# The second MoE stage's two projections as Strassen's seven block products over 384-token halves

## The chip, the cores and the metric

The kernel runs on one core of a Trainium2 chip. Five engines of the core work side by side and wait for each other through semaphores: TensorE (PE) multiplies matrices and writes the sums into PSUM, eight banks of 512 float32 columns on 128 partitions; VectorE (DVE) and ScalarE (ACT) do elementwise work and can read and write PSUM; GpSimd (POOL) does elementwise work in SBUF only; SyncE (SP) issues the DMAs. The metric is the time on the device in microseconds (us), less is better.

## What is computed

Attention over 2 x 768 tokens, then two MoE layers, each with one dense expert. The change touches only the second of them:

```python
def _moe_ref(x, w_in, w_out):           # 1536 tokens, 512 -> 2048 -> 512
    h = x @ w_in
    g = np.where(h >= 1, h, np.where(h <= -1, 0.0, (h + 1) ** 2 / 4.0))
    return (g @ w_out).astype(np.float32)

def _moe2_ref(x, w_gate, w_val, w_out): # 1536 tokens, 512 -> 1536 -> 512
    gate = 1.0 / (1.0 + np.exp(-(x @ w_gate)))
    val = x @ w_val
    return (gate * val @ w_out).astype(np.float32)
```

The weights come as float64. Every factor of a matmul is split in two float32r parts, a high one (the rounded value) and a low one (what the rounding lost), and a product is high x high + high x low + low x high: three matmuls for one.

## The kernel before

The attention part (`banded`, line 571 on) works on tiles of 112 queries; the first MoE layer's first stage runs between its tiles. After it comes `moe` (line 562): for each layer, each stage and each block of `TOK` = 512 tokens it calls `block` (line 404). A stage is a group of hidden chunks of 128 columns: four stages of four chunks in layer 1, four of three in layer 2 (`STAGES`, line 26). "The second stage" in this text means layer 2 as a whole.

`block` in layer 2 does this for each of its three chunks `f`: `proj("wg", f)` and `proj("wv", f)` each issue 12 matmuls of 512 columns (four 128-row parts of the model dimension times three products, lines 437 to 439) into one bank; ACT takes the sigmoid of the gate's bank (line 469); DVE multiplies it with the value's bank (line 472); the result is split into `gh` (a copy, lines 291, 293 or 295 by engine) and `gl` (a subtraction, line 298). Then the back projection: for each of four 128-token tiles, three chunks times three matmuls (lines 521 to 523), and a sum into `acc` in SBUF (line 536). In the last stage each finished tile is written out by a DMA of SP (line 546).

`load` (line 342) brings a weight chunk: a DMA of the float64 bits into `st`, then ACT rescales the high words (362), DVE clamps (365), shifts (368), restores the sign (371) and appends the low bits (374), and the chunk is split into its high and low part. Nineteen slots hold split chunks (`N_EARLY`, `N_LATE`), more than two stages of layer 2 need, so that later chunks are loaded while earlier ones are in use.

At the end of layer 1 the finished `acc` of a block is split into `xh` and `xl` (lines 540 to 543), on which layer 2 works.

The order of all this isn't the order of the calls. Every step is handed to a planner (`Plan`, line 117) with the engines that can do it, a duration for each, a due time, and what it reads and writes. `order` (line 158) runs through time: whenever an engine is free, it starts the step with the earliest due time among those that are ready and for whose new buffers there is room. `self.due` counts PE's work; elementwise steps get the due time of their matmul less `DRAIN` = 3.77. The instructions are then issued in that order; nothing is decided at run time, and each engine takes its instructions strictly in order. Buffers come from rings (`Ring`): all PSUM rings share the eight banks, and a ring of `n` buffers gives out buffer `i` when buffer `i - n` is done.

Of the kernel before, what the change touches and what calls it, by code (L numbers as in the profile page):

```python
# [25 lines left out]
STAGES = {1: (4, 4, 4, 4), 2: (3, 3, 3, 3)}  # L26
GROUPS = (512, 1024, 1536)
N_EARLY = 8
N_LATE = 19 - N_EARLY
G_BUFS = 6  # L30
PR_BUFS, PTS_BUFS, V_BUFS, C_BUFS = 6, 6, 6, 2
SC_BANKS, OT_BANKS, PT_BANKS, O_BANKS, H_BANKS = 4, 1, 2, 4, 5

# [65 lines left out]
class Ring:  # L99


    def __init__(self, n, make, banks=None):
        self.n, self.make, self.asked, self.taken, self.banks = n, make, [], 0, banks

# [12 lines left out]
class Plan:  # L117
# [40 lines left out]
    def order(self):  # L158
# [13 lines left out]
        running = []  # L172

        def room(o, t):
# [8 lines left out]
            return all(len(idle(b.ring.banks, t)) >= len(o.new) for b in o.new if b.ring.banks)  # L183
# [4 lines left out]
        def idle(banks, t):  # L188

            ends = [(0.0 if b is None else max(u.end for u in b.users), i) for i, b in enumerate(banks) if b is None or over(b, t)]  # L190
            return [i for _, i in sorted(ends)]
# [10 lines left out]
        while done < len(self.ops):  # L202
# [13 lines left out]
            for e in engines:  # L216
# [9 lines left out]
                for b in o.new:  # L226
                    b.ring.taken += 1
                    if b.ring.banks:
                        b.bank = idle(b.ring.banks, now)[0]
                        b.ring.banks[b.bank] = b  # L230
                t = begin(o, e)
# [14 lines left out]
    def run(self):  # L246
        order, end = self.order()
        for o in order:
            for b in o.new:
                b.ap = b.ring.make(b.bank) if b.ring.banks else b.ring.make()  # L250
            o.fn(o.eng) if o.pick else o.fn()
        return end


class Body:


    def __init__(self, ctx, tc, a, out, pre):
# [4 lines left out]
        self.stages = {}  # L263
        for layer, f in ((1, a["w1"].shape[0]), (2, a["wg"].shape[0])):
            ends = [sum(STAGES[layer][:i + 1]) for i in range(len(STAGES[layer]))]
            assert ends[-1] == f
            self.stages[layer] = [range(e - n, e) for e, n in zip(ends, STAGES[layer])]
# [3 lines left out]
        slots = self.pool(ctx, "w1p")  # L271
        self.early = [self.slot_tiles(slots, i) for i in range(N_EARLY)]
        g, tmp, wst = self.pool(ctx, "g"), self.pool(ctx, "tmp"), self.pool(ctx, "wst")
# [4 lines left out]
        ring = lambda pool, n, shape, dt, tag: Ring(n, lambda: pool.tile(shape, dt, tag=tag, name=tag, bufs=n))  # L278
        self.g_r = [ring(g, G_BUFS, [P, TOK], F32R, t) for t in ("gh", "gl")]
        self.t_r = [ring(tmp, 2, [P, TOK], F32, t) for t in ("r", "v")]  # L280
        self.o_r = self.bank_ring(O_BANKS)
        self.st_r = ring(wst, 3, [P, 512, 2], I32, "st")
        self.c_r, self.w_r = ring(wst, C_BUFS, [P, 512], F32, "c"), ring(wst, 2, [P, 512], F32, "w")
        self.h_r = self.bank_ring(H_BANKS)
        self.due = 0.0
        self.att_end = None
        self.weights()
# [20 lines left out]
    def bank_ring(self, n, parts=P, *shape):  # L308
# [9 lines left out]
        return Ring(n, view, self.banks)  # L318

    def slot_tiles(self, pool, i):  # L320
        return tuple(pool.tile([P, 512], F32R, name=f"w{x}{i}") for x in "hl")

    def later(self):
        if self.late is None:
            self.att.close()
            self.late = {"w": self.pool(self.ctx, "w2p")}
            self.late["slots"] = [self.slot_tiles(self.late["w"], N_EARLY + i) for i in range(N_LATE)]
        return self.late


    def weights(self):

        self.units, self.first = [], {}
        for layer, into, back in ((1, ("w1",), "w2"), (2, ("wg", "wv"), "wo")):
            for fs in self.stages[layer]:
                for nm, f in [(nm, f) for f in fs for nm in into] + [(back, f) for f in fs]:
# [677 lines left out]
```

## Time and profile before

| | |
|---|---|
| median of 3 runs | 658.73 us (657.57 to 660.29) |
| the profiled execution's span | 657.5 us |
| PE, DVE, ACT, POOL busy | 98%, 67%, 43%, 6% of the span |
| instructions | 9228, of them 3373 matmuls and 3373 weight loads |
| mean granted TensorE clock | 0.996 of 2.4 GHz |

A profile is one execution, taken by the hardware's profiler; its span goes from the first to the last instruction. A view by lines groups instructions; "idle before" is the time in which the engine waited for them, with what released it. Matmuls are pipelined: their recorded durations overlap, so their pace is the distance of their starts, which the view in order of time gives. DVE's and ACT's records overlap a little for the same reason.

### The profile page before, as it was taken

The page shows a single profiled execution, that of the slowest core. Times are in us where ns is not written, and L with a number is a line of the kernel's source. Part 1 is how long each engine was busy: PE and PEld are TensorE (multiplying, and loading weights), DVE is VectorE, ACT ScalarE, POOL GpSimd, SP SyncE. Part 2 cuts the span into 40 slices and gives each one's busy share as a digit, 9 for nine tenths or more (in the row PEclk, how much of TensorE's full clock was granted, in tenths as well). Part 3 has the DMA queues.
Part 4 walks back from the last instruction along what each step waited for, and adds up shares of the span by engine and source line. Part 5 has one row for each costly group of instructions (what it writes and reads, how often), then busy time and mean ns, then how long its engine had stood idle before and what let it go on. Part 6 is the DMA issues. An engine that isn't in the chain of part 4 may idle for free.

```text
span 657.5 us, 9228 instructions
## 1 busy us (share of the span) xinstructions
PE 645.8 (98%) x3373; PEld 527.9 (80%) x3373; DVE 439.0 (67%) x955; ACT 283.6 (43%) x614; POOL 40.3 (6%) x49
## 2 busy tenths in 40 slices
PE   8999999999999999999999999999999999999996
PEld 5677777888888888888888888888888888888885
DVE  5799998799998895789788902973278222222322
ACT  5899988556553442344445422441133111111110
POOL 0021111001010000000001100000000000000000
PEclk9899999999999999999999999999999999999999
DMA  6677555142443221122012300340011000001012
GB/s 189 204 224 214 165 171 167 33 146 80 160 129 96 97 94 34 33 96 97 32 33 96 123 7 0 127 147 16 0 44 55 0 1 0 1 0 65 1 64 69
DMA packets 28566, 54.43 MB, mean 83 GB/s; under 512 B 3296, under 2 KB 18400, under 8 KB 28512
## 3 DMA queue, kind: packets, MB, share of 16 engines
q1 hardware_dynamic: 28512, 53.75, 25.6%
q8 instruction: 28, 0.46, 0.3%
q14 instruction: 26, 0.21, 0.1%
HBM read 50.60 MB, written 3.15 MB: 82 GB/s over the span
## 4 chain that ended last, share of the span: by engine, by line
PE 90%; DVE 7%; DMA 1%; ACT 1%; issue 0%; DVEq 0%; ACTq 0%
PE bank L437 16%; PE bank L439 16%; PE bank L438 16%; PE bank L517 7%; PE bank L519 7%; PE bank L518 7%; PE bank L522 5%; PE bank L523 5%; PE bank L521 5%; PE bank L648 2%; DVE pr L651 2%; PE bank L688 2%; PE bank L665 2%; DMA qk<-in_qk 1%; DVE xl L298 1%; PE bank L711 0%
## 5 line engine op out<-in xcount | busy, mean ns | idle before, releaser
L437 PE MATMUL bank<-xh,wh 128*128 128x512 f32 x480 | 188.0, 392 | 0.0
L438 PE MATMUL bank<-xl,wh 128*128 128x512 f32 x480 | 187.1, 390 | 0.1
L439 PE MATMUL bank<-xh,wl 128*128 128x512 f32 x480 | 187.0, 390 | 0.0
L291 ACT ACTIVATE gh<-v 128x512 fp32r<-128x512 f32 x81 | 51.2, 632 | 137.8 <-DVE v L472 114.2
L437 PEld LDWEIGHTS bank<-xh,wh 128*128 128x128 f32 x480 | 90.2, 188 | 19.0 <-issue 0.3
L438 PEld LDWEIGHTS bank<-xl,wh 128*128 128x128 f32 x480 | 90.2, 188 | 18.8 <-DVE xl L298 0.4
L439 PEld LDWEIGHTS bank<-xh,wl 128*128 128x128 f32 x480 | 90.2, 188 | 18.7
L472 DVE TENSOR_TENSOR v<-r,bank 128x512 f32<-128x512 f32 x36 | 24.7, 686 | 104.1 <-PE bank L439 104.1
L536 DVE TENSOR_TENSOR acc<-bank,acc 128x512 f32<-128x512 f32 (+1 forms) x73 | 49.1, 683 | 44.2 <-PE bank L523 31.4
L517 PE MATMUL bank<-gh,wh 128*128 128x512 f32 x192 | 75.5, 393 | 0.0
L519 PE MATMUL bank<-gh,wl 128*128 128x512 f32 x192 | 74.8, 390 | 0.0
L518 PE MATMUL bank<-gl,wh 128*128 128x512 f32 x192 | 74.8, 390 | 0.0
L298 DVE TENSOR_TENSOR gl<-v,gh 128x512 fp32r<-128x512 f32 x83 | 57.0, 687 | 19.1 <-ACT gh L291 19.0
L362 ACT ACTIVATE c<-st 128x512 f32<-128x512 f32 x68 | 45.5, 671 | 33.1 <-DVE w L371 9.8
L657 ACT ACTIVATE pr<-pr,mx 112x256 f32<-112x256 f32 (+2 forms) x112 | 54.0, 487 | 10.5 <-DVE mx L651 10.1
L523 PE MATMUL bank<-wh,gl 128*128 128x512 f32 (+1 forms) x147 | 56.6, 385 | 0.0
L522 PE MATMUL bank<-wl,gh 128*128 128x512 f32 (+1 forms) x147 | 56.6, 385 | 0.0
L521 PE MATMUL bank<-wh,gh 128*128 128x512 f32 (+1 forms) x147 | 56.6, 385 | 0.0
L291 ACT ACTIVATE wh<-w 128x512 fp32r<-128x512 f32 x53 | 33.3, 630 | 48.3 <-PE bank L438 18.9
L469 ACT ACTIVATE r<-bank 128x512 f32<-128x512 f32 x36 | 21.5, 597 | 61.4 <-PE bank L439 61.3
L371 DVE SCALAR_TENSOR_TENSOR w<-c,w 128x512 int32<-128x512 int32 x68 | 47.7, 707 | 0.3
L374 DVE SCALAR_TENSOR_TENSOR w<-st,w 128x512 int32<-128x512 int32 x68 | 46.9, 693 | 0.4
(87 smaller groups left out, 770.4 us busy)
## 6 DMA issues: line engine op xcount, KB each, us to landing
st<-in_w SPq DMA_DIRECT2D x32, 512.0 KB, 3.4
qk<-in_qk SPq DMA_DIRECT2D x56, 128.0 KB, 2.8
v<-in_vb SPq DMA_DIRECT2D x52, 128.0 KB, 3.2
st<-in_wg SPq DMA_DIRECT2D x12, 512.0 KB, 3.3
st<-in_wv SPq DMA_DIRECT2D x12, 512.0 KB, 3.3
st<-in_wo SPq DMA_DIRECT2D x12, 512.0 KB, 3.3
out<-acc SPq DMA_DIRECT2D x11, 256.0 KB, 2.1
acc<-in_qk SPq DMA_DIRECT2D x4, 128.0 KB, 2.7
```

What stands on the lines that cost most here:

```text
L291: self.nc.scalar.activation(out=out, in_=x, func=AF.Copy)
L298: (self.nc.vector if e == "DVE" else self.nc.gpsimd).tensor_tensor(out=out, in0=x, in1=y, op=ALU.subtract)
L437: mm(out=out, lhsT=wh[:, c], rhs=mh, start=k == 0, stop=False)
L438: mm(out=out, lhsT=wh[:, c], rhs=ml, start=False, stop=False)
L439: mm(out=out, lhsT=wl[:, c], rhs=mh, start=False, stop=k == KD - 1)
L517: mm(out=out, lhsT=wh[:, c], rhs=gh, start=first, stop=False)
L518: mm(out=out, lhsT=wh[:, c], rhs=gl, start=False, stop=False)
L519: mm(out=out, lhsT=wl[:, c], rhs=gh, start=False, stop=last)
L521: mm(out=out, lhsT=gh[:, c], rhs=wh[:, c0:c1], start=first, stop=False)
L522: mm(out=out, lhsT=gh[:, c], rhs=wl[:, c0:c1], start=False, stop=False)
L523: mm(out=out, lhsT=gl[:, c], rhs=wh[:, c0:c1], start=False, stop=last)
L657: nc.scalar.activation(out=pr.ap[:n, e, :ks * P], in_=pr.ap[:n, e, :ks * P], func=AF.Exp, bias=mx.ap[:n, e:e + 1], scale=-1.0, accum_out=s ...
```

## The change

The x of the second stage (512 model dimensions by 1536 tokens) is cut into two groups of 768 tokens, and each group into four blocks: two halves of the model dimension by two halves of 384 tokens. A pair of hidden chunks of a weight (512 by 256) is cut into four blocks as well. A product of two 2 by 2 block matrices takes eight block products; Strassen's form (in Winograd's variant) takes seven, of sums and differences of blocks.

- `quarters` forms the seven x blocks (`11`, `21`, `22` as they are, `T1` to `T4` as differences) from `acc` and splits each in high and low.
- `load` for a pair of chunks forms the seven weight blocks (`PART`) by four additions and subtractions of 256 columns on DVE or POOL and splits them.
- `seven` issues the products, each 6 matmuls of 384 columns (two 128-row parts times three), in four banks A, B, D, E. Instead of adding in SBUF at the end, it copies a partial sum from a bank to another bank (A to B after product 1, B to E after product 4) and lets the next product accumulate on top; D goes to SBUF (`keep`) and is added by DVE where a result needs it (`total`). The copies may run on ACT or DVE.
- `gated` strings gate and value calls of both token groups and the back projection (`back`, two chunks per sum instead of three) together; there are six pairs instead of four stages of three chunks.
- The weights of a pair have one place each (`PAIR_AT`, `BACK_AT`); the separate buffer `c` of the weight path is gone (`w` is worked on in place).
- Bank rings are marked: B and E may only take a bank that was last written in its full width.

Layer 1's stages, the attention part and the number of weight bytes are as before; layer 1 has 17 weight slots in place of 19.

```diff
@@ constants
-STAGES = {1: (4, 4, 4, 4), 2: (3, 3, 3, 3)}
+HT = 384
+TP = 2 * HT
+STAGES = (4, 4, 4, 4)
-N_EARLY = 8
-N_LATE = 19 - N_EARLY
+E_SLOTS, L_SLOTS = 8, 9
-PR_BUFS, PTS_BUFS, V_BUFS, C_BUFS = 6, 6, 6, 2
+G_BUFS, GT_BUFS = 6, 6
+R_BUFS, K_BUFS = 8, 4
+PR_BUFS, PTS_BUFS, V_BUFS, W_BUFS = 6, 6, 6, 4
+A_BANKS, B_BANKS, D_BANKS, E_BANKS = 2, 2, 2, 2
+PART = {"11": 0, "12": 256, "S3": 512, "22": 768, "S1": 1024, "S2": 1280, "S4": 1536}
+PAIR_AT = {"wg": ("e", 0), "wv": ("e", 2 * N_PART)}
+BACK_AT = ((("e", 28), ("e", 30)), (("g", 18), ("g", 20)))
...
@@ Plan.order
-            return [i for _, i in sorted(ends)]
+            return [i for _, i in sorted(ends) if whole[i] or not ring.seeded]
...
@@ Body.load, for a pair of chunks
+        u1, u2 = (self.raw(self.a[nm][2 * i + j], due) for j in range(2))
+        s = Buf(self.w_r)
+        split(lambda: u1.ap, PART["11"], D, [u1])
+        mix((s, a), (u2, a), (u2, b), ALU.add, [u2], s)
+        mix((s, b), (s, a), (u1, a), ALU.subtract, [u1], s)
+        mix((u2, a), (u1, a), (u2, a), ALU.subtract, [u1], u2)
+        mix((u1, b), (u1, b), (s, b), ALU.subtract, [s], u1)
+        split(lambda: u2.ap, PART["S3"], D, [u2])
+        split(lambda: s.ap, PART["S1"], D, [s])
+        split(lambda: u1.ap[:, b], PART["S4"], D // 2, [u1])
...
@@ Body.quarters, for each of the two 128-row parts i of a half
+            b11, b12, b21, b22 = sums(i, u), sums(i, v), sums(2 + i, u), sums(2 + i, v)
+            t1, t2 = temp(), temp()
+            split(b11, "11")
+            less(t1, b12, b11)
+            split(t1, "T1")
+            split(b21, "21")
+            less(t2, b22, t1)
+            split(t2, "T2")
+            split(b22, "22")
+            less(b12, b22, b12)
+            less(b21, b21, t2)
+            rest += [lambda x=b12, split=split: split(x, "T3"), lambda x=b21, split=split: split(x, "T4")]
...
+    def seven(self, nm, p, b, take):
+        A, D = Buf(self.a_r), Buf(self.d_r)
+        B, E = Buf(self.b_r), Buf(self.e_r)
+        keep = Buf(self.k_r)
+        pick = lambda: {"ACT": a_us(HT), "DVE": d2_us(HT)}
+        after = self.turn if p == 0 else ()
+
+        def product(o, part, x, start):
+            self.due += us
...
+                for i in range(2):
+                    c = slice(PART[part] + i * P, PART[part] + (i + 1) * P)
+                    for n, (w, m) in enumerate(((wh, hi(i)), (wh, lo(i)), (wl, hi(i)))):
+                        nc.tensor.matmul(out=out, lhsT=w[:, c], rhs=m, start=start and i == n == 0, stop=i == 1 and n == 2, skip_group_check=True)
...
+            op("PE", us, self.due, go, keys, [o], after=self.past if p == 0 else ())
+            return self.due - DRAIN
+
+        t = product(A, "11", "11", True)
+        op(pick(), 0, t, lambda e: self.copy(e, cut(B), cut(A)), [A], [B])
+        t = product(D, "S1", "T1", True)
+        op(pick(), 0, t, lambda e: self.copy(e, keep.ap, cut(D)), [D], [keep], after=after)
+        t = product(A, "12", "21", False)
+        take(0, 0, lambda: cut(A), [A], t)
+        t = product(B, "S2", "T2", False)
+        op(pick(), 0, t, lambda e: self.copy(e, cut(E), cut(B)), [B], [E])
+        t = product(E, "S4", "22", False)
+        take.summed(0, 1, E, keep, t)
+        t = product(B, "S3", "T3", False)
+        take.summed(1, 1, B, keep, t)
+        t = product(B, "22", "T4", False)
+        take(1, 0, lambda: cut(B), [B], t)
...
+    def gated(self, p):
+        def total(x, o, k, due):
+            op("DVE", d2_us(HT), due, lambda: nc.vector.tensor_tensor(out=x.ap, in0=cut(o), in1=k.ap, op=ALU.add), [o, k], [x], after=after)
+        class Gate:
+            def __call__(self, i, j, x, keys, due, r=None):
+                r = r or Buf(body.r_r)
+                gates[self.b, i, j] = r
+                op("ACT", a_us(HT), due, lambda: nc.scalar.activation(out=r.ap, in_=x(), func=AF.Sigmoid), keys, [r], after=after)
+            def summed(self, i, j, o, k, due):
+                r = Buf(body.r_r)
+                total(r, o, k, due)
+                self(i, j, lambda: r.ap, [], due, r)
...
+        class Value(Gate):
+            def __call__(self, i, j, x, keys, due, on=None):
+                r, gh, gl = gates[self.b, i, j], Buf(body.gt_r[0]), Buf(body.gt_r[1])
+                g[self.b, i, j] = gh, gl
+                f = lambda e: body.mix(e, r.ap, r.ap, x(), ALU.mult)
+                op({"DVE": d2_us(HT), "POOL": g2_us(HT)} if on else {"DVE": d2_us(HT)}, 0, due, f, keys, [r])
+                body.halves(lambda: r.ap, HT, lambda: gh.ap, lambda: gl.ap, [gh], [gl], due, [r], after)
+            def summed(self, i, j, o, k, due):
+                x = Buf(body.k_r)
+                total(x, o, k, due)
+                self(i, j, lambda: x.ap, [x], due, True)
...
+        def back(b):
+            for j in range(TP // P):
...
+                    o = Buf(self.o_r)
...
+                    for i in range(2):
+                        k, x = self.W("wo", 2 * p + i, t)
+                        tiles.append((g[b, i, j // 3], x))
...
+        for f, b in ((gate, 0), (value, 0), (gate, 1), (back, 0), (value, 1), (back, 1)) if p == 0 else ((gate, 0), (gate, 1), (value, 0), (back, 0), (value, 1), (back, 1)):
+            f(b)
...
@@ Body.moe
+                if s == len(self.stages) - 1 and t:
+                    rest += self.quarters(t // TOK - 1)
+        for x in rest:
+            x()
+        for p in range(self.pairs):
+            self.gated(p)
```

`self.past` are the last block's projections of layer 1, `self.turn` its back projections: the first pair's products come after the first, the steps that reuse layer 1's buffers after the second.

## Rows read from the trace of the kernel before

**Rows 1.** the page's busy time by engine: us, share of the span, instructions
```profile
PE 645.8 (98%) x3373; PEld 527.9 (80%) x3373; DVE 439.0 (67%) x955; ACT 283.6 (43%) x614; POOL 40.3 (6%) x49
```

**Rows 2.** the page's chain that ended last: shares of the span by engine
```profile
PE 90%; DVE 7%; DMA 1%; ACT 1%; issue 0%; DVEq 0%; ACTq 0%
```

**Rows 3.** stretches: length, busy us (instructions) of PE, PEld, DVE, ACT, POOL, clock, DMA
```profile
125.00:355.00 230.00, 230.00 (x1017) 190.57 (x1016) 201.95 (x357) 108.31 (x174) 14.89 (x11) 1.00 0.27 87
175.00:200.00 25.00, 25.00 (x112) 20.72 (x111) 24.86 (x45) 14.09 (x23) 3.74 (x3) 1.00 0.40 124
500.00:600.00 100.00, 100.00 (x442) 82.84 (x442) 32.55 (x50) 16.01 (x26) 0.00 (x0) 1.00 0.00 1
```

**Rows 4.** the last block in order of time: start, us, engine, line
```profile
639.67 0.39 PE L439 MATMUL bank<-xh,wl 128*128 128x512 f32 x1
...
649.42 0.28 PE L521 MATMUL bank<-wh,gh 128*128 128x256 f32 x1
...
651.45 0.28 PE L523 MATMUL bank<-wh,gl 128*128 128x256 f32 x1
...
651.77 0.42 DVE L536 TENSOR_TENSOR acc<-bank,acc 128x256 f32<-128x256 f32 x1 [0.29 <-PE bank L523]
```

**Rows 5.** weight loads and matmuls by line: count, busy us, mean ns
```profile
L521 PEld LDWEIGHTS bank<-wh,gh 128*128 128x128 f32 x147 | 27.6, 188 | 5.6
...
L521 PE MATMUL bank<-wh,gh 128*128 128x256 f32 x6 | 1.7, 282 | 0.0
```

**Rows 6.** elementwise operations by line and form: count, busy us, mean ns
```profile
L291 ACT ACTIVATE pts<-bank 128x384 f32<-128x384 f32 x5 | 2.2, 481 | 1.3 <-PE bank L665 1.3
...
L293 DVE COPY pts<-bank 128x384 f32<-128x384 f32 x3 | 1.6, 546 | 0.0
...
L536 DVE TENSOR_TENSOR acc<-bank,acc 128x512 f32<-128x512 f32 x71 | 48.2, 690 | 43.1 <-PE bank L523 30.3 <-PE bank L519 12.7
...
L536 DVE TENSOR_TENSOR acc<-bank,acc 128x256 f32<-128x256 f32 x2 | 0.8, 424 | 1.0 <-PE bank L523 1.0
...
L368 DVE TENSOR_SCALAR w<-c 128x512 int32<-128x512 int32 x68 | 29.8, 443 | 0.6
...
L362 ACT ACTIVATE c<-st 128x512 f32<-128x512 f32 x68 | 45.5, 671 | 33.1 <-DVE w L371 9.8
...
L291 ACT ACTIVATE wh<-w 128x512 fp32r<-128x512 f32 x53 | 33.3, 630 | 48.3 <-PE bank L438 18.9
```

**Rows 7.** a gate's last steps in order of time (DVE, ACT, DVE)
```profile
639.49 0.69 DVE L472 TENSOR_TENSOR v<-r,bank 128x512 f32<-128x512 f32 x1 [3.36 <-PE bank L439]
...
640.21 0.63 ACT L291 ACTIVATE gh<-v 128x512 fp32r<-128x512 f32 x1 [4.21 <-DVE v L472]
...
640.88 0.69 DVE L298 TENSOR_TENSOR gl<-v,gh 128x512 fp32r<-128x512 f32 x1 [0.70 <-ACT gh L291]
```

**Rows 8.** DVE alone in order of time, in a full stretch
```profile
176.58 0.68 DVE L459 TENSOR_TENSOR v<-r,bank 128x512 f32<-128x512 f32 x1
177.18 0.68 DVE L453 TENSOR_SCALAR r<-bank 128x512 f32<-128x512 f32 x1
...
179.91 0.41 DVE L368 TENSOR_SCALAR w<-c 128x512 int32<-128x512 int32 x1
180.25 0.41 DVE L365 TENSOR_SCALAR c<-c 128x512 f32<-128x512 f32 x1
```

**Rows 9.** POOL and DVE in order of time, while POOL runs a split
```profile
361.74 1.80 POOL L298 TENSOR_TENSOR wl<-w,wh 128x512 fp32r<-128x512 f32 x1 [1.10 <-ACT wh L291]
...
362.91 0.92 DVE L368 TENSOR_SCALAR w<-c 128x512 int32<-128x512 int32 x1
```

**Rows 10.** stretches of the attention part, columns as in rows 3
```profile
16.00:22.00 6.00, 4.91 (x32) 2.59 (x30) 4.71 (x22) 5.41 (x21) 0.56 (x1) 0.93 0.95 315
22.00:30.00 8.00, 8.00 (x75) 5.84 (x74) 5.86 (x26) 6.67 (x21) 0.56 (x1) 0.84 0.52 149
30.00:40.00 10.00, 9.16 (x114) 7.34 (x113) 9.93 (x39) 9.89 (x33) 1.35 (x2) 1.00 0.72 234
```

More of the change, by code (lines that the diff above doesn't have):

```diff
@@ new lines, in held, with mix, halves @@
+    def held(self, place, c, n):
+        where, cell = place
+        return [(where, i) for i in range(cell + c // CELL, cell - (-(c + n) // CELL))]
+    def mix(self, e, out, x, y, alu):
+        (self.nc.vector if e == "DVE" else self.nc.gpsimd).tensor_tensor(out=out, in0=x, in1=y, op=alu)
+    def halves(self, x, n, hi, lo, hk, lk, due, reads, after=()):
+        hp = self.plan.op({"ACT": a_us(n), "DVE": d1_us(n), "POOL": g1_us(n)}, 0, due, lambda e: self.copy(e, hi(), x()), reads, hk, after=after)
+        lp = self.plan.op({"DVE": d2_us(n), "POOL": g2_us(n)}, 0, due, lambda e: self.less(e, lo(), x(), f32v(hi())), [*reads, *hk], lk, after=after)
+        return hp, lp
@@ new lines, in pieces, with mms @@
+            def pieces(h=h, r=r, v=v):
+                nc.vector.tensor_tensor(out=c(v), in0=c(r), in1=c(h), op=ALU.max)
+            op("DVE", d2_us(n), t - DRAIN, inner, [h], [r])
+            op("ACT", a_us(n), t - DRAIN, square, [], [r])
+            op("DVE", d2_us(n), t - DRAIN, pieces, [h, r], [v])
+            self.halves(lambda v=v: c(v), n, lambda gh=gh: c(gh), lambda gl=gl: c(gl), [gh], [gl], t - DRAIN, [v])
+        banks = [Buf(self.o_r) for _ in range(KD)]
+        def mms(d, part, t):
+            o = banks[d]
@@ L548, in block @@
[L548 to L568 removed]
+                    mm(out=out, lhsT=wh[:, c], rhs=gh, start=f == fs[0], stop=False)
@@ new lines, in go, with after @@
+                    mm(out=out, lhsT=wh[:, c], rhs=gl, start=False, stop=False)
+                    mm(out=out, lhsT=wl[:, c], rhs=gh, start=False, stop=f == fs[-1])
+            x = op("PE", 3 * len(part) * mm_us, t, go, keys, [o])
+            if end and t0 + n == self.NT:
+                self.turn.append(x)
+        def after(d, t):
+            o = banks[d]
+            a0 = d * self.NT + t0
+            c = self.acc[:, a0:a0 + n]
+            k = cells("acc", 0, a0, a0 + n)
+            if s == 0:
+                op({"ACT": a_us(n), "DVE": d2_us(n)}, 0, t - DRAIN, lambda e: self.copy(e, c, o.ap[:, :n]), [o], k)
+            else:
+                op("DVE", d2_us(n), t - DRAIN, lambda: nc.vector.tensor_tensor(out=c, in0=o.ap[:, :n], in1=c, op=ALU.add), [o], k)
```

382 lines of the change are left out of this document (218 added, 164 removed).

## The prediction

> **What bounds the kernel now.** I read the busy table first: TensorE (PE) is busy 98% of the span, VectorE (DVE) 67%, ScalarE (ACT) 43% [rows 1]. A busy PE is not yet a bound, so next the chain that ended last: 90% of it is PE and only 7% DVE [rows 2]. Then the stretches: from 125 to 355 us and in the later stretches read PE has no idle time, at granted clock 1.00, both where DVE is nearly full (24.86 of 25 us, 175 to 200 us) and where it is a third full (500 to 600 us) [rows 3]. The second MoE stage therefore lasts as long as its matmuls take to issue, and everything else in it is cover.
>
> The pace is read from starts, not from the 0.39 us that a matmul lasts. From 639.67 to 649.42 us lie 43 matmuls of 512 columns: 9.75/43 = 0.2267 us each. From 649.42 to 651.45 us lie 17 of 256 columns: 2.03/17 = 0.1194 us [rows 4]. So a column costs (0.2267 - 0.1194)/256 = 0.419 ns and an instruction about 12 ns besides; both are full clock (2.4 GHz).
>
> **The change, part by part.**
>
> *Matmuls of the two projections.* Before: 12 chunks x 3 blocks x 24 = 864 of 512 columns, 864 x 0.2267 = 195.9 us. After: 7 products x 6 matmuls x 2 weights x 2 halves x 6 pairs = 1008 of 384 columns. No row has 384; it lies midway between the two measured widths, so (0.2267 + 0.1194)/2 = 0.1731 us, and 174.5 us in all. Bounds: 0.1194 and 0.2267. **-21.4 us.** The back projection keeps its 432 matmuls (72 x 0.2267 = 16.3 us per pair); a product is 6 x 0.1731 = 1.04 us; a pair of chunks is 28 x 1.04 + 16.3 = 45.4 us on PE.
>
> A weight load lasts 188 ns [rows 5], longer than 173. It would matter if loads couldn't overlap; but the 256-column matmuls go at 119 ns with the same 188 ns loads between them [rows 4, 5], so I count no cost. The Trainium skill ("TensorE: Matmul & The Clock Gate", Back-to-back issue gap) speaks against the change: it gives a sustained 81 ns at 128 columns and 131 ns at 512 in a stream of loads and matmuls. Interpolated, that is 115 ns at 384, an estimate: 1008 x 0.115 = 115.9 against 864 x 0.131 = 113.2 us, a loss of 2.7 us. The trace disagrees, at 227 and 119 ns for 512 and 256 columns, and I go by it.
>
> *Handovers on PE's path.* The seven products of one call are no longer independent. Product 5 adds onto a bank that is copied from another bank after product 4; product 7 writes the bank that DVE must have read after product 6. (The first copy has the second product in front of it.) What is queued behind such a wait is all of PE, in order. The price of one: DVE starts 0.20 us after PE is free (last start 651.45 + 0.12, DVE at 651.77) [rows 4]; a 384-column read of a bank takes 0.481 us on ACT, 0.546 on DVE [rows 6]; an engine follows another after about 0.04 us (640.84 to 640.88) [rows 7]; then a weight load, 0.19 us. Sum 0.91 on ACT, 0.98 on DVE. No row shows a write from bank to bank; the copy of 384 columns may cost less than 0.48 or, at the worst, as much as two such reads, 0.96. I take 0.48, the nearest row. There are 24 calls, so 24 x (0.91 + 0.98) = 45.4 us if nothing lay beside it. What hides it: the next call's first and second product (1.04 us each) depend on nothing in this call, two banks of each kind are there, and the planner starts any step that is ready. One product just covers one handover, with 0.06 to 0.13 us to spare; a longer wait in ACT's or DVE's queue takes a second filler (another product, or a back tile of 1.36 us). Bounds 0 to 16 us for 23 calls; I take **+3 us**.
>
> *DVE.* The issue spacing of a 512-column operation is 0.60 us, of the two-times-faster forms 0.33 us [rows 8]; so 384 columns about 0.47 and a 256-column mix 0.33 (estimates from these). Per pair: 24 gate, value and split operations x 0.47 = 11.3; 12 sums into acc x 0.60 = 7.2 (two chunks per sum in place of three); weights 6 x (0.33 + 0.33 + 0.60 + 0.60) = 11.2; 8 mixes x 0.33 = 2.6; low parts 6 x 0.60 + 2 x 0.33 + 2 x 0.60 = 5.5. Sum 37.8 us of 45.4, or 83%. Before, two chunks needed (6 + 6 + 8) x 0.60 + 6 x 2.46 = 26.8 us of 49. Cover for 83%: from 175 to 200 us 45 operations filled DVE's rows completely, and PE lost nothing [rows 3]. GpSimd is little help: while it ran a split, a DVE operation of 0.44 us took 0.92 [rows 6, 9]. ACT, counted with whole durations, has 28 operations x 0.48, 6 rescales x 0.67 and high parts of 8 x 0.63 + 2 x 0.39 us [rows 6], 23.3 of 45.4 us: free enough. No charge beyond the 3 us above; the worst case is a rival.
>
> *Weights are no longer double-buffered.* The next pair's gate matrix can be written after this pair's second gate call; value, back, value, back lie before its use: 14.5 + 16.3 = 30.8 us of PE for 7.2 us of DVE. The value matrix has 8.2 + 14.5 = 22.7 us. SP issues the same 36 loads. Cost 0; if the cover went, some us per pair.
>
> *The turn between the stages.* 40 additions and splits of the x quarters x 0.47 = 18.8 us of DVE replace 12 low parts (7.2). The first half runs under the last block's 21.8 us of PE. The second must follow that block's last sum, about 9.4 us, while the first gate and value calls have 14.5 us of PE work, part of it stuck until DVE has read their banks. **+1.5 us** (0 to 8).
>
> *The end.* The very last call has no next call to hide its handovers: 0.91 + 0.98. After its seventh product the back tiles need a split: sum, multiply, high, low, about 0.8 us after it. **+2.7 us** (1 to 4). The output tail of 6 us stays.
>
> *Removed besides.* The separate buffer c, two weight slots: 0, with ±1.5 us for a reshuffled order before 125 us.
>
> Sum on the profiled execution: 657.5 - 21.4 + 3 + 1.5 + 2.7 = 643.3 us. The median of the runs is 1.2 us above that span, so **644.5 us**.
>
> **Rivals.**
> (a) *DVE becomes the bound.* If operations cost their whole durations instead of their spacing (0.55 for 384 columns, 0.69 for 512, 0.42 for 256, 0.44 for the fast ones [rows 6]) with 0.04 us between each of 78, a pair needs 44.9 + 3.1 = 48.0 us against PE's 45.4: 2.6 x 5 pairs = 13 us in place of the 3. For it: 83% on average, chains of dependent steps. Against: [rows 3]. About 654.5 us.
> (b) *Handovers lie open*, the slower case: products wait at the bank copies because ACT's or DVE's queue is late and the filler is already spent. It decides at 21.4 - 1.5 - 0.8 = 19.1 us, 42% of the 45.4; with 60% open it is 27.2, and 657.5 - 21.4 + 27.2 + 2.3 + 1.2 = 667 us. For it: cover exceeds price by only a tenth of a microsecond. Against: PE waits in none of the stretches of [rows 3], though each block's gates have such chains.
> In this case the clock could fall too: the granted mean was 0.93 and 0.84 (between 2.4 and 1.2 GHz) from 16 to 30 us, where PE had idled 1.1 us among short matmuls, yet 1.00 from 30 to 40 us with 0.84 us idle [rows 10]; 16% of 8 us is 1.3 us an episode. The Trainium skill (same page, A second HAM failure mode) says that stepping through banks with small idles makes the clock swing; rows 10 agree at one place and not at the next.
> (c) *The narrower matmul isn't cheaper*: it does not do what it says. At the weight load's 188 ns, 1008 x 0.188 = 189.5 us, a gain of 6.4 and, with the losses, 659.5 us. Against: 119 ns at 256 columns. The Trainium skill's figures above would be this case at its extreme.
> (d) *Weights or quarters come late* once or in every pair: 8 us more, about 652 us.
> (e) *No handover shows*: 638 to 640 us.
>
> **How the numbers follow.** Forecast (640 to 649) 0.62, (a) 0.15, (b) 0.10, (c) 0.03, (d) 0.04, (e) 0.06. The range leaves out (b), most of (c) and the far part of (a), some 2 in 10: 638 to 655.5 us. A measurement of this kernel can tell about 0.5%, 3.3 us, from no change: 655.4 to 662.0 is "same". Faster 0.62 + 0.06 + 0.11 of (a) + 0.03 of (d) = 0.82; same 0.04 of (a), 0.02 of (b), 0.02 of (c), 0.01 of (d) = 0.09; slower 0.08 of (b) and 0.01 of (c) = 0.09.
>
> **What would show it.** Starts of 384-column matmuls 0.17 us apart (c: 0.19 or more). PE idle in the second stage of about 7 us in all, most of it at the turn and in the last call; (b) shows idle before products 5 and 7 of many calls, released by ACT or DVE copies; (a) shows DVE rows without gaps for 200 us while PE waits for sums or splits; (d) shows PE's weight loads waiting for splits of weights or x. Clock 1.00 throughout. I am wrong if PE's idle time is over 19 us, or if the stage's matmuls don't fall by 21 us.

## The result and the profile after

| kernel | median, us | range of the runs, us | ratio to before (95% interval) | profiled span, us |
|---|---|---|---|---|
| before | 658.80 | 657.57 to 660.29 | 1 | 657.5 |
| changed | 643.89 | 643.14 to 645.48 | 0.9774 (0.9753 to 0.9795) | 642.3 |

The changed kernel is 2.3% faster. 644.5 us was forecast, with 638 to 655.5 as the range. The sum comes out, but not every term of it does, and the experiments say which.

The page of the changed kernel, busy time by engine and the chain by engine (they answer to [rows 1, 2]):

```profile
PE 625.5 (97%) x3514; PEld 540.8 (84%) x3514; DVE 520.6 (81%) x1137; ACT 316.1 (49%) x723; POOL 80.8 (13%) x94
...
PE 89%; DVE 6%; ACT 3%; issue 1%; POOL 0%; ACTq 0%; POOLq 0%; DVEq 0%
```

There are 141 matmuls more on record (144 more in the projections, and 3 fewer because the last tile, which is issued in two halves, sums two chunks in place of three) and 20 us less of PE. DVE does 82 us more. The chain is PE's as before, so the change moved work onto DVE and left the bound where it was.

Stretches of the changed kernel: length, then busy us (instructions) of PE, PEld, DVE, ACT and POOL, the granted clock, DMA share and GB/s (they answer to [rows 3]):

```profile
0.00:125.00 125.00, 116.61 (x1013) 91.15 (x1014) 108.32 (x387) 100.80 (x321) 15.81 (x31) 0.96 0.60 184
355.00:637.00 282.00, 278.91 (x1457) 258.46 (x1455) 222.08 (x417) 121.21 (x245) 41.75 (x40) 1.00 0.17 57
400.00:600.00 200.00, 200.00 (x1052) 186.99 (x1051) 166.63 (x314) 85.54 (x173) 34.83 (x34) 1.00 0.18 59
```

From 400 to 600 us, nearly four and a half pairs of chunks, PE has no idle time at all, and DVE is 166.63/200 = 83% busy. In the whole second stage PE idles 282 - 278.91 = 3.1 us. Before 125 us it idles 8.4 us, and in the kernel before it idled 125 - 119.05 = 5.95 there:

```profile
0.00:125.00 125.00, 119.05 (x1042) 91.24 (x1043) 106.35 (x385) 102.23 (x321) 18.21 (x33) 0.99 0.58 176
```

The pace, from starts of PE in order of time in the changed kernel (start, us, engine, line; it answers to [rows 4]):

```profile
374.30 0.33 PE L669 MATMUL bank<-xh,early 128*128 128x384 f32 x1
...
380.54 0.68 PE L669 MATMUL bank<-late,early 128*128 128x384 f32 x3
```

36 matmuls of 384 columns start between these two: 6.24/36 = 0.1733 us each, and 0.1731 was forecast. The weight load of 188 ns between them costs nothing.

PE's waits in the second stage of the changed kernel (what it waited for: us in total, times, longest). Only these three of the list lie there:

```profile
PE bank L669 <- ACT bank L322: 1.5, 1, 1.5
...
PE bank L752 <- ACT gs L322: 0.9, 1, 0.9
PE bank L669 <- DVE tmp L699: 0.7, 1, 0.7
```

The first is at the turn between the stages, the other two at the end: in the last call, and before the last back tiles. Of the 72 bank handovers of 24 calls, two are in this list in the whole kernel. A third shows in the starts alone: PE, in step until 381.58, starts a product at 381.67, 0.05 us after the end of the bank copy that it waits for, and loses 0.2 us there with the slow start behind it (ACT and PE in order of time):

```profile
381.13 0.49 ACT L322 ACTIVATE bank<-bank 128x384 f32<-128x384 f32 x1
...
381.67 0.44 PE L669 MATMUL bank<-xh,early 128*128 128x384 f32 x1
```

The changed kernel was run again beside the experiments:

> The changed kernel once more, beside the next three: 643 to 645 us. Its PE idle times of the second stage should come again at the same places (1.7 us at the turn, 0.8 and 1.05 us in the last call); the stretches of lower granted clock before 60 us may come at others.

643.72 us, 0.9777 (0.9764 to 0.9791), and the same three waits at the same places with the same lengths.

**Where the 15.2 us of span went.** Matmuls: 864 x 0.2267 - 1008 x 0.1733 = 195.9 - 174.7 = -21.2. The turn: starts 370.26 and 372.09 (below), 1.83 less the pace, +1.66. The last call: 0.67 open and some 0.16 hidden in a longer record, +0.83; then 627.68 to 628.97 in place of 0.23, +1.05. The remainder of the second stage: the stage, counted as if nothing of it had been mixed into layer 1, runs from 365.20 less the 36 early matmuls (6.24), which is 358.96, to 636.80, so 277.8 us, of which 174.7 + 432 x 0.2267 = 272.6 is pace; 277.8 - 272.6 - 1.66 - 0.83 - 1.05 = +1.6; the slow starts right behind the three waits and the 0.2 us at 381.67 make 0.66 of it, the rest is small and at no one place. Attention and layer 1: before, the last matmul of layer 1 ended its turn at 363.14 with 24 matmuls of the second stage in front (5.44), so 357.70; now 358.96, +1.26. This term belongs to the one execution that was profiled and not to the kernel: in the second trace of the same kernel layer 1 ends at 364.15 - 6.24 = 357.91, +0.21 (e7 takes it up). The second stage is 277.8 us long in both traces. The tail after the last matmul start is 0.4 shorter. Sum -21.2 + 1.66 + 1.88 + 1.6 + 1.26 - 0.4 = -15.2.

The rows for the 24 and the 36 count matmuls up to the last one of layer 1. Columns are the length, PE and PEld busy (instructions), clock, DMA share and GB/s. First the kernel before, line L437, the first of three lines (200 matmuls, 192 of them layer 1's, so 8 threes of the second stage); then line L669 of the changed kernel:

```profile
0.00:363.10 363.10, 79.00 (x200) 37.76 (x201) 1.00 0.37 117
```

```profile
0.00:365.19 365.19, 6.61 (x36) 6.52 (x37) 0.99 0.33 104
```

The same line in the second trace of the changed kernel, and the first start of PE after layer 1 there:

```profile
0.00:364.13 364.13, 6.61 (x36) 6.52 (x37) 0.99 0.33 104
```

```profile
364.15 1.23 PE L669 MATMUL bank<-late,early 128*128 128x384 f32 x6
```

### The profile page after: what moved, and what is told of

Its sections match the earlier page's. It is cut to its first block, busy times and chain, and to the rows that moved or that the text cites. A ratio compares the mean times of both kernels' runs of the same rounds, so it can differ in the third digit from the quotient of the medians.

```text
span 642.3 us, 9817 instructions
## 1 busy us (share of the span) xinstructions
PE 625.5 (97%) x3514; PEld 540.8 (84%) x3514; DVE 520.6 (81%) x1137; ACT 316.1 (49%) x723; POOL 80.8 (13%) x94
## 4 chain that ended last, share of the span: by engine, by line
PE 89%; DVE 6%; ACT 3%; issue 1%; POOL 0%; ACTq 0%; POOLq 0%; DVEq 0%
PE bank L669 26%; PE bank L558 7%; PE bank L560 7%; PE bank L559 7%; PE bank L513 6%; PE bank L515 6%; PE bank L514 6%; PE bank L754 5%; PE bank L752 5%; PE bank L753 5%; PE bank L863 3%; PE bank L903 2%; DVE pr L866 2%; PE bank L880 2%; ACT pr L872 2%; PE bank L926 1%
## 5 line engine op out<-in xcount | busy, mean ns | idle before, releaser
L669 PE MATMUL bank<-xh,early 128*128 128x384 f32 x384 | 107.7, 335 | 1.5 <-ACT bank L322 1.5
L669 PE MATMUL bank<-late,early 128*128 128x384 f32 x432 | 85.3, 335 | 0.7 <-DVE tmp L699 0.7
L669 PEld LDWEIGHTS bank<-late,early 128*128 128x128 f32 x432 | 76.0, 188 | 1.5 <-DVE tmp L699 1.0
L669 PEld LDWEIGHTS bank<-xh,early 128*128 128x128 f32 x384 | 70.2, 188 | 2.4 <-ACT bank L322 2.1
L669 PE MATMUL bank<-xl,early 128*128 128x384 f32 x192 | 64.2, 334 | 0.0
L416 ACT ACTIVATE w<-st 128x512 f32<-128x512 f32 x68 | 44.7, 666 | 16.2 <-DMA st<-in_w 10.3
L425 DVE SCALAR_TENSOR_TENSOR w<-st,w 128x512 int32<-128x512 int32 x68 | 46.8, 692 | 0.6
L428 DVE SCALAR_TENSOR_TENSOR w<-st,w 128x512 int32<-128x512 int32 x68 | 46.7, 690 | 0.4
L866 DVE CUSTOM_DVE_ANT_0 pr<-bank,mask 112x256 f32<-112x256 f32 (+2 forms) x112 | 39.4, 395 | 4.1 <-PE bank L863 4.0
L513 PE MATMUL bank<-xh,early 128*128 128x512 f32 x96 | 38.8, 404 | 0.0
L558 PE MATMUL bank<-gs,early 128*128 128x512 f32 x96 | 38.2, 397 | 0.0
L515 PE MATMUL bank<-xh,early 128*128 128x512 f32 x96 | 37.5, 391 | 0.0
L560 PE MATMUL bank<-gs,early 128*128 128x512 f32 x96 | 37.4, 390 | 0.0
```

Of the source, the lines that this page charges most:

```text
L425: nc.vector.scalar_tensor_tensor(out=t(), in0=high(), scalar=-0x80000000, in1=t(), op0=ALU.bitwise_and, op1=ALU.bitwise_or)
L428: nc.vector.scalar_tensor_tensor(out=t(), in0=low(), scalar=29, in1=t(), op0=ALU.logical_shift_right, op1=ALU.bitwise_or)
L513: mm(out=out, lhsT=wh[:, c], rhs=mh, start=k == 0, stop=False)
L515: mm(out=out, lhsT=wl[:, c], rhs=mh, start=False, stop=k == KD - 1)
L558: mm(out=out, lhsT=wh[:, c], rhs=gh, start=f == fs[0], stop=False)
L560: mm(out=out, lhsT=wl[:, c], rhs=gh, start=False, stop=f == fs[-1])
```

## Experiments

| label | edit | median, us | ratio to before (95% interval) |
|---|---|---|---|
| e1_serial | a call may not start before the last one's end | 703.84 | 1.0691 (1.0668 to 1.0713) |
| e8_eight | eight plain products, no copies, no sums of blocks | 664.59 | 1.0100 (1.0083 to 1.0117) |
| e3_dve_copies | bank copies on DVE alone | 647.56 | 0.9844 (0.9827 to 0.9860) |
| e7_weight_path | before, with the new weight path alone | 659.31 | 1.0022 (1.0002 to 1.0042) |
| e4_table | ACT's table loaded ahead of the turn | 643.31 | 0.9758 (0.9745 to 0.9772) |
| e5_last | other order of calls in the last pair | 641.34 | 0.9750 (0.9727 to 0.9773) |
| e6_both | e4 and e5 | 641.17 | 0.9735 (0.9718 to 0.9751) |
| e9_turn_split | e6, one split kept off POOL | 640.08 | 0.9720 (0.9697 to 0.9744) |
| e10_no_pool | e6, nothing of the second stage on POOL | 640.04 | 0.9713 (0.9686 to 0.9741) |

All but e7 are edits of the changed kernel.

**Is the cover real? (e1)** The forecast had nearly all of 45.4 us of handovers hidden by the next call's products. Here the first product of each call waits for the last one of the call before.

```diff
-            op("PE", us, self.due, go, keys, [o], after=self.past if p == 0 else ())
+            x = op("PE", us, self.due, go, keys, [o], after=[*(self.past if p == 0 else ()), *self.prior])
+            self.prior = []
+            self.newest = x
...
         take(1, 0, lambda: cut(B), [B], t)
+        self.prior = [self.newest]
```

> Every call's first product must wait for the previous call's last product; nothing else changes. My theory: the handovers before product 5 and product 7 cost about 0.91 and 0.98 us each and are hidden by the next call's first products. With those taken away 24 calls x 1.89 = 45 us come into the open, less what back tiles still cover (two of the four calls of a pair have back tiles beside them, so perhaps 10 to 20 us): 644 + 25 to 45, 669 to 689 us, with PE idle before products 5 and 7 of most calls. Rival: handovers are short or overlap with the products themselves, and the time stays under 650 us. Second rival: back tiles cover all, 645 to 650 us.

It took 60 us more than the changed kernel, well over what either theory expected. PE's waits on the seven products, and one of them in order of time:

```profile
PE bank L669 <- ACT bank L322: 30.4, 43, 1.6
PE bank L669 <- DVE rest L702: 7.8, 7, 2.8
...
PE bank L669 <- ACT xh L322: 2.1, 1, 2.1
PE bank L669 <- DVE tmp L702: 2.0, 3, 0.7
...
PE bank L669 <- DVE xl L329: 0.4, 1, 0.4
```

```profile
433.96 0.34 PE L669 MATMUL bank<-xh,early 128*128 128x384 f32 x1
434.39 0.47 ACT L322 ACTIVATE bank<-bank 128x384 f32<-128x384 f32 x1 [0.61 <-PE bank L669]
434.92 0.44 PE L669 MATMUL bank<-xh,early 128*128 128x384 f32 x1 [0.62 <-ACT bank L322]
...
435.20 0.33 PE L669 MATMUL bank<-xl,early 128*128 128x384 f32 x1
```

55 waits, 42.7 us. A wait hides more than its bracket says: the last matmul before it is on record for 0.33 us where its pace is 0.17 (0.16 lost), and the first after it takes 0.28 to the next start in place of 0.17 (0.11 lost). 55 x 0.27 = 14.9, together 57.6. One ACT handover is thus 434.92 - 433.96 - 0.17 + 0.11 = 0.90 us, and 443.98 - 443.08 - 0.17 + 0.11 = 0.84 where the copy starts soonest; the forecast had 0.91. The clock adds some: from 365 to 400 us PE idled 8 us and the granted clock was 0.90 (between the levels 1.2 and 2.4 GHz). Part of that fell into idle time; 14 matmuls between the waits start 0.32 us apart in place of 0.17, 2.1 us.

```profile
365.00:400.00 35.00, 27.07 (x123) 23.48 (x122) 24.65 (x48) 18.65 (x37) 3.24 (x3) 0.90 0.05 16
```

Less the 2.7 us of the same kind that the changed kernel has, these make 57.0 of the 60. The expectation was too low since my edit opened more than the two handovers it meant to: the second product of a call isn't bound by it, goes ahead as filler elsewhere, and then the first copy, from A to B, has nothing in front of it either. The waits bear this out: 43 of the 55 are for a bank copy on ACT, and by what the product in front of each copy reads (product 4 reads T2, which lies in `late`; product 1 doesn't) 22 of these are the first copy and 21 the second; only 10 are for DVE to read a bank. So the price per handover was right and so was the mechanism: the slower rival (b) isn't excluded by cheap handovers but by the order alone. Without the cover this kernel would be 7% slower than the one before.

**What are the seven products worth? (e8)** The same pairs, halves and places, with eight products, each block of the result in its own bank; copies, block sums of weights and of x fall away.

```diff
-        t = product(A, "11", "11", True)
-        op(pick(), 0, t, lambda e: self.copy(e, cut(B), cut(A)), [A], [B])
...
+        for o, i, j in ((A, 0, 0), (D, 0, 1), (E, 1, 1), (B, 1, 0)):
+            product(o, ("11", "S3")[i], ("11", "12")[j], True)
+            t = product(o, ("12", "22")[i], ("21", "22")[j], False)
+            take(i, j, lambda o=o: cut(o), [o], t)
```

> The same pairs of chunks, 384-token halves, weight places and order, but the plain eight block products, each result in a bank of its own: no copies from bank to bank, no sums of blocks of x or of weights. 144 more matmuls of 384 columns at 0.1733 us are +25.0 us; the two gaps that are handovers of the last call (about 1 us in all) and the quarter differences fall away. My theory (PE's matmul count sets the time): 643.9 + 25.0 - 1 to 3 = 666 to 668 us, some 8 us above the kernel before, since 384 columns pay the fixed 12 ns more often (1152 x 0.1733 = 199.6 against 195.9 us) and the turn remains. Rival (DVE or the weights bound the changed kernel as much as PE does): with that work gone the added matmuls are partly free, 650 to 660 us.

664.59 us. PE lost nothing in the steady stretch, DVE fell to 65%:

```profile
400.00:600.00 200.00, 200.00 (x1064) 188.47 (x1063) 129.30 (x229) 57.57 (x106) 9.62 (x11) 1.00 0.17 56
```

So seven products in place of eight, with all the copies and sums that this takes, are worth 664.6 - 643.9 = 20.7 us, of 144 matmuls x 0.1733 = 25.0 that it saves. The rest of the edit, halves of 384 in place of blocks of 512, costs 5.8 us against the kernel before: 1152 x 0.1733 - 195.9 = 3.7 is the 12 ns per instruction that narrower matmuls pay more often, the other 2.1 hold one open split at the end (0.6) and slow starts that I did not take apart. The earlier stages have no part in it: layer 1 ends at 357.73 us there, 357.70 in the kernel before.

**Who should copy? (e3)** All 72 copies (48 from bank to bank, 24 to SBUF) on DVE, which was the fuller engine.

```diff
-        pick = lambda: {"ACT": a_us(HT), "DVE": d2_us(HT)}
+        pick = lambda: {"DVE": d2_us(HT)}
```

> The three copies of each call (two from bank to bank, one to SBUF) may run on DVE alone instead of ACT or DVE. That adds up to 72 x 0.47 = 34 us to DVE in the second stage, 5.6 us per pair: 37.8 + 5.6 = 43.4 of 45.4 us. My theory: DVE stood at about 83% and still has room: 644 to 648 us, PE idle up to 5 us. Rival (DVE already at its bound): each added microsecond shows, 660 to 678 us.

3.7 us slower than the changed kernel, and the turn holds nearly all of it:

```profile
PE bank L669 <- DVE rest L699: 3.7, 1, 3.7
```

```profile
365.00:380.00 15.00, 11.17 (x52) 10.25 (x51) 13.52 (x28) 8.37 (x16) 2.26 (x2) 0.89 0.00 0
400.00:600.00 200.00, 200.00 (x1052) 186.67 (x1051) 188.55 (x353) 72.55 (x136) 38.72 (x39) 1.00 0.18 59
```

At the turn PE idled 15 - 11.17 = 3.8 us, 2.3 more than in the changed kernel (13.50 busy of the same 15), and the granted clock was 0.89: ten matmuls from 375.84 us on start 0.32 us apart in place of 0.17, another 1.5. The steady stretch stands DVE at 94% without a wait of PE. That speaks against rival (a) more strongly than the forecast could: DVE's share of the time isn't what decides, as long as PE has a choice of products. At the turn it has none, and there the wait for DVE showed.

**Where do the earlier stages lose 1.3 us? (e7)** The kernel before with the new weight path alone (buffer c gone, four slots for w in place of two and two; the sign taken from the raw weight).

```diff
-PR_BUFS, PTS_BUFS, V_BUFS, C_BUFS = 6, 6, 6, 2
+PR_BUFS, PTS_BUFS, V_BUFS, W_BUFS = 6, 6, 6, 4
...
-        op("DVE", d1_us(512), due, shift, [c], [w], port=True)
-        op("DVE", d2_us(512), due, sign, [c, w], [w], port=True)
+        op("DVE", d1_us(512), due, shift, [], [w], port=True)
+        op("DVE", d2_us(512), due, sign, [st], [w], port=True)
```

> The kernel before with only the new weight path: no buffer c, w worked on in place, four buffers w, the sign read from st. In the changed kernel layer 1 ends 1.3 us later than before once the second stage's matmuls in front of it are taken off. Theory 1: the reshuffled order of weights and attention costs it: about +1 us, 659 to 661 us, and PE's idle time before 125 us rises from 6.0 to about 8 us. Theory 2: the weight path is neutral (other slots, or the lower clock of that stretch, made the difference): 658 to 659 us, idle as before.

659.31 us, 0.0022 x 659 = 1.4 us over the kernel before on the same chip; the interval only just leaves 1 out. The eight executions fall into two groups, five from 658.7 to 659.4 and three from 661.4 to 662.8 us, and the profile is of one of the three (661.82). Its first 125 us show the idle time of the changed kernel, 8.6 us, and not that of the kernel before:

```profile
0.00:125.00 125.00, 116.37 (x999) 90.70 (x1000) 107.90 (x386) 100.35 (x319) 15.80 (x31) 0.95 0.59 184
```

PE's waits say where. For copies of `ie` on POOL it waits 2.4 us in e7 and 2.2 in the changed kernel, 0.7 before; for one of `pts` on DVE 1.1 in both, 0.2 before. So the idle time comes with the weight path, or with the order that the planner makes of it. The +1.3 does not follow from it. Layer 1's end, found as above in every trace, beside the granted clock of the first 60 us:

| clock, 0 to 60 us | layer 1 ends at, us |
|---|---|
| 0.97 | before 357.70, e9 358.10 |
| 0.94 | changed kernel, second trace, 357.91; e3 358.17, e5 357.55, e8 357.73 |
| 0.91 | changed kernel, first trace, 358.96; e6 358.80, e10 359.05, e4 362.15 |
| 0.89 | e1 360.34, e7 360.81 |

The clock of the stretch in the kernel before and in the two traces of the changed kernel:

```profile
0.00:60.00 60.00, 54.81 (x476) 40.74 (x478) 48.64 (x200) 48.74 (x160) 7.85 (x21) 0.97 0.70 211
```

```profile
0.00:60.00 60.00, 52.02 (x453) 38.85 (x454) 49.05 (x193) 45.61 (x152) 9.85 (x24) 0.91 0.69 210
```

```profile
0.00:60.00 60.00, 52.07 (x459) 38.70 (x460) 49.07 (x196) 46.61 (x155) 10.75 (x24) 0.94 0.68 204
```

All but the first entry have the new weight path, and the end goes with the clock (e4 also has 1.0 us of waits for a DMA in that part). At the clock of the kernel before, e9 is 0.4 us later; that much may be the weight path's. Whole executions don't contradict it: at a mean clock of 0.988 the kernel before took 661.42 us and e7 661.82 and 661.36; at 0.991 the kernel before took 659.39 and 659.57 and e7 659.38 and 662.76. Theory 1 is thus shown for PE's idle time and not for the time of the kernel. What sets the clock in one execution or another stays open, and so does what the slots that were taken away add.

**What holds PE at the turn? (e4)** ACT, DVE, POOL and PE in order of time at the turn of the changed kernel:

```profile
368.34 1.31 POOL L329 TENSOR_TENSOR gs<-w,gs 128x512 fp32r<-128x512 f32 x1 [1.67 <-ACT gs L322]
...
368.35 1.20 PE L669 MATMUL bank<-late,early 128*128 128x384 f32 x6
...
368.42 1.64 DVE L329 TENSOR_TENSOR xl<-acc,xh 128x384 fp32r<-128x384 f32 x1
...
369.05 1.28 ACT L708 ACT_TABLE_LOAD   x1
...
370.26 0.34 PE L669 MATMUL bank<-xh,early 128*128 128x384 f32 x1
...
371.14 0.51 ACT L322 ACTIVATE late<-tmp 128x384 fp32r<-128x384 f32 x1
...
371.56 0.48 ACT L322 ACTIVATE bank<-bank 128x384 f32<-128x384 f32 x1
...
372.09 0.44 PE L669 MATMUL bank<-xh,early 128*128 128x384 f32 x1 [1.50 <-ACT bank L322]
```

The bank copy of 371.56 reads what the product of 368.35 wrote (product 4 of its call, whose T2 lies in `late`); that ended at 368.35 + 1.20 = 369.55, so the copy could have begun at about 369.6. The product behind it, whose last matmul starts at 370.26, is the filler: it covers one handover, but ACT came 1.9 us late. In ACT's queue stands a load of the sigmoid's table, 1.28 us. The first theory was that load. The edit asks for one sigmoid of one element just after layer 1's last square, so that the load falls into idle time of ACT.

```diff
-            op("ACT", a_us(n), t - DRAIN, square, [], [r])
+            x = op("ACT", a_us(n), t - DRAIN, square, [], [r])
+            if end and t0 + n == self.NT and f == fs[-1]:
+                s1 = self.pre["scratch"]
+                op("ACT", 1.5, t + 3.0, lambda: nc.scalar.activation(out=s1, in_=s1, func=AF.Sigmoid), after=[x])
```

> A sigmoid of one element on ACT right after the last square of layer 1, so that the sigmoid table is loaded under layer 1's last back projections instead of at the turn, where its 1.28 us stand in front of a copy from bank to bank. My theory: the 1.7 us gap of PE at the turn goes: 642.2 to 642.6 us against 643.9. Rival: DVE's and ACT's work on the x blocks is what is late there, and a gap of 1 us or more stays: 643.3 to 644.

643.31 us: 0.6 less than the changed kernel, and within the intervals no difference. The profiled execution took 646.91 us, the longest of the six; its layer 1 ends 3.2 us later, and so the turn comes later. The wait fell from 1.5 to 0.9 us, start to start from 1.83 to 1.27. The theory was half wrong. What is left, in order of time in this kernel:

```profile
371.53 1.31 POOL L329 TENSOR_TENSOR gs<-w,gs 128x512 fp32r<-128x512 f32 x1 [1.66 <-ACT gs L322]
...
371.61 1.65 DVE L329 TENSOR_TENSOR xl<-acc,xh 128x384 fp32r<-128x384 f32 x1
...
373.18 0.55 DVE L371 TENSOR_TENSOR tmp<-acc,rest 128x384 f32<-128x384 f32 x1
...
373.76 0.52 ACT L322 ACTIVATE late<-tmp 128x384 fp32r<-128x384 f32 x1 [0.73 <-DVE tmp L371]
...
374.19 0.47 ACT L322 ACTIVATE bank<-bank 128x384 f32<-128x384 f32 x1
...
374.71 0.44 PE L672 MATMUL bank<-xh,early 128*128 128x384 f32 x1 [0.93 <-ACT bank L322]
```

The copy that PE needs stands in ACT's queue behind a high part; that waits for a subtraction on DVE; that stands in DVE's queue behind a low part that takes 1.65 us in place of 0.55, beside a split on POOL. The bank itself had long been ready.

**The end (e5, and e6 with both).** In the last pair, back tiles stood ahead of the second value call, so nothing was left to lie beside its last products.

```diff
+        final = ((gate, 0), (gate, 1), (value, 0), (value, 1), (back, 0), (back, 1))
...
+        for f, b in first if p == 0 else final if last else other:
```

> In the last pair both value calls come before both back projections, so that back tiles can fill the handovers of the last value call. My theory: the gaps of 0.8 and 1.05 us in the last call are open because nothing else is left to do, so they go: about 1.5 to 1.9 us less, 642.0 to 642.4. Rival: the rings of gate buffers (6) stop the last call earlier in that order, and the time stays or grows by 1 to 2 us.

641.34 us, 2.5 less than the changed kernel. Both waits of the last call are gone (of the three above only the one at the turn is listed). They were 1.88 us of it, and the second stage takes 276.0 us in place of 277.8. The other 0.6 lies outside the stage, where two traces of one kernel differ by more. What they were, in the changed kernel, PE, DVE and ACT in order of time:

```profile
625.46 0.55 DVE L699 TENSOR_TENSOR tmp<-bank,tmp 128x384 f32<-128x384 f32 x1
...
626.06 1.32 PE L669 MATMUL bank<-late,early 128*128 128x384 f32 x6 [0.67 <-DVE tmp L699]
...
628.39 0.52 ACT L322 ACTIVATE gs<-tmp 128x384 fp32r<-128x384 f32 x1 [1.15 <-DVE tmp L371]
...
628.97 0.50 PE L752 MATMUL bank<-gs 128*128 128x512 f32 x1 [0.88 <-ACT gs L322]
```

> Both edits together. If the gaps are independent they add: about 3.4 us less than the changed kernel, 640.3 to 641 us.

641.17 us; the wait of 0.9 at the turn is the one that stays. The medians of e5 and e6 don't tell the two apart. The length of the second stage does, counted as above: 277.8 us in both traces of the changed kernel, 277.3 in e4, 276.0 in e5, 275.5 in e6. The two gains add.

**The chain at the turn, tested (e9, e10).** If POOL's split stretches DVE's operation and that holds up ACT's queue, the turn must close when that one split goes elsewhere.

```diff
+        if self.nopool:
+            del ho["POOL"], lo_on["POOL"]
...
+            self.nopool = nm == "wo" and i == 1
```

> The version with both edits (table early, last pair reordered), and besides the split of the second back weight, which becomes free at the turn, on DVE alone instead of POOL. At the turn POOL's split ran from 371.53 to 372.84 us in the run with the early table, and a DVE subtraction beside it took 1.65 us instead of 0.55; ACT stood behind that with its next split, the copy from bank to bank behind ACT's split, PE behind the copy. My theory: that 1.1 us is most of the 0.9 us of PE idle that is left, so the gap at the turn falls to 0.3 us or less and the time by about 0.6 us, 640.2 to 640.8. Rival: the order of ACT's queue alone holds the copy, and the gap stays near 0.9.

640.08 us, and no wait of the seven products is left in the list. The same places in order of time:

```profile
367.56 0.55 DVE L329 TENSOR_TENSOR xl<-acc,xh 128x384 fp32r<-128x384 f32 x1
...
368.87 0.53 ACT L322 ACTIVATE late<-tmp 128x384 fp32r<-128x384 f32 x1
...
369.28 0.49 ACT L322 ACTIVATE bank<-bank 128x384 f32<-128x384 f32 x1
```

The low part takes 0.55 us again, and PE's start-to-start gap there is 0.43 in place of 1.27: 0.84 of the 1.1 us that the whole kernel gained. That last figure is itself inside the spread of the runs; the rows carry the verdict, not the medians. The second stage takes 274.4 us, 1.1 less than in e6.

> The version with both edits, but with nothing of the second stage on POOL: about 40 operations (some 42 us of POOL time) go to DVE and ACT, about 30 of them to DVE at 0.33 to 0.60 us, 15 us more on DVE over 275 us. My theory: POOL's work costs DVE about as much as it saves, since DVE operations stand still beside it, so the time stays within 1 us of the version with both edits (640.2 to 642.2). Rival: POOL is real help, DVE at 83% plus 5% begins to be late, and the time rises by 2 us or more.

640.04 us. With POOL empty in the steady stretch, DVE rises from 165.94 (e6) to 172.98 us and PE loses nothing:

```profile
400.00:600.00 200.00, 200.00 (x1052) 187.01 (x1051) 172.98 (x347) 85.48 (x169) 0.00 (x0) 1.00 0.18 59
```

34.8 us of work on POOL had spared DVE 7.0 us, and PE nothing. Both kernels are faster than the one before (2.8 to 2.9%) and 3.8 us below the changed kernel.

## Why the prediction was right

- **The bound and the matmuls.** PE's pace was the bound and stayed it. 0.1733 us at 384 columns against 0.1731, -21.2 against -21.4. Rival (c) falls, and with it the pace interpolated from the Trainium skill ("TensorE: Matmul & The Clock Gate", Back-to-back issue gap), an estimate of 115 ns (its two figures give 114).
- **Handovers, +3 forecast.** The price was right (0.84 to 0.90 on ACT against 0.91, e1; 0.83 + 0.11 = 0.94 for DVE's read in the last call against 0.98), and the cover too, better than I dared: no wait from 400 to 600 us. What the rows tie to this term is the 0.2 us at 381.67; with all the slow starts it would be 1.6. The term was too large. Rival (b) had the right price and the wrong share: 2 of 72 open, and those are charged to the turn and the end.
- **DVE, no charge.** 83% forecast, 83% measured, but not like for like: the forecast had all 78 operations of a pair on DVE, and the planner gave about 8 of them to POOL. With POOL empty (e10) DVE has 347 operations in 200 us, 79 a pair, and 86%. Operations go at their spacing, as [rows 8] said, not at their durations as in rival (a). e3 shows PE without a wait at 94%.
- **Weights single-buffered, 0.** PE's list has no wait for a weight split; rival (d) falls.
- **The turn, +1.5 forecast, +1.66 measured, by another cause.** I sized it as DVE's backlog of quarters, and banks unread. The measured wait was for a bank copy in ACT's queue, held up by the table load (a third, e4) and by a chain POOL to DVE to ACT (the rest, e9). Neither was in the sum, though [rows 9] showed the stretched operation. The agreement of the size is luck.
- **The end, +2.7 forecast, +1.9 measured.** I charged both handovers of the last call and the split. Only that of product 7 lay open; back tiles of the first half stood in front of product 5 and hid its copy. The split (0.8 forecast) was 1.05.
- **Removed besides, 0 ± 1.5, measured +1.26 in one trace and +0.21 in the other.** That is the spread between executions, which goes with the clock of the attention part; the weight path can be 0.4 of it (e7).
- **PE's idle time, about 7 us forecast,** was 3.1, or 5.2 if the slow starts count. Most of it lies at the turn and at the end, as forecast.

So the total is within 0.6 us partly because errors cancel: in the first trace handovers -1.4 or more, the end -0.8 and the tail -0.4 on one side, the earlier stages +1.3 on the other. The second stage alone went from 293.87 us (357.70 to 651.57) to 277.84 (358.96 to 636.80; 277.83 in the second trace), 16.0 less, where the sum had 21.4 - 3 - 1.5 - 2.7 = 14.2 less.

## What to carry to other kernels

A block scheme with fewer products pays on a kernel bound by PE when the chains that it makes can lie beside independent products: 24 chains of three handovers cost two open ones here, and 60 us when the next call was held back. Price one handover (0.9 us) times their number first, then look where the supply of independent work ends: at the first and the last call, which took all of the waits. A copy that PE waits for is only as early as the queue of the engine it is put on; look in that queue for table loads and for operations that wait on a third engine. Before a microsecond is put down to an edit, trace the same kernel twice: here the stretch ahead of the change moved by 1.05 us between two traces, and the changed stage by none.

## What the runs showed of the hardware

- **A copy from bank to bank costs what a read of a bank costs**: on ACT 475 ns, on DVE 566 ns at 128x384, against 481 and 546 for a bank read into SBUF in [rows 6]. Operations of the changed kernel by line and form (min/median/max in ns):

```profile
L322 ACT ACTIVATE bank<-bank x44: 469/475/488, 350.2 to 615.2; 128x384 f32<-128x384 f32 x44
L324 DVE COPY bank<-bank x4: 566/566/567, 351.3 to 563.3; 128x384 f32<-128x384 f32 x4
```

- **PE restarts slowly.** After a wait its first two matmuls start 0.28 us apart in place of 0.17 (372.09 to 372.37 at the turn, 434.92 to 435.20 in e1). A wait costs about 0.27 us more than its bracket.
- **POOL and DVE.** A subtraction of two SBUF tiles on DVE took 1.64 us beside a POOL split in place of 0.55, and 0.55 again when that split was gone (e9). It ended about 0.4 us after the split did (370.06 and 369.65 at the turn, 373.26 and 372.84 in e4). The Trainium skill ("SBUF — State Buffer", Who interferes with whom) says that a DVE instruction with two SBUF inputs contends with a GpSimd instruction that reads SBUF; the trace agrees.
- **The clock after a long wait.** 0.89 from 365 to 380 us in e3, where PE had idled 3.8 us, and 0.90 from 365 to 400 us in e1, with 8 us idle; 1.00 over the whole second stage of the changed kernel, which has the three single waits. In the attention part it differs from one execution to the next: 0.91 and 0.94 over the first 60 us in the two traces of the changed kernel, and layer 1 ends 1.05 us apart (e7). No experiment was made on it.
